# Relu and square of the summed quarters of fast up-projections, as two instructions or as one on VectorE

## The chip, the cores and the metric

The kernel runs on one core of a Trainium2 chip. The metric is the device time of one execution in microseconds (us). The engines are TensorE (PE, with its weight loads as PEld), VectorE (DVE), ScalarE (ACT), GpSimd (POOL) and SyncE (SP).

## The reference

Sliding-window attention with a linear position bias, followed by a feed-forward block whose activation is the square of a relu. There are 8 batches of 576 tokens, 8 heads of 64, a window of 128 keys, 2048 hidden features; inputs and output are f32.

```python
scores = scale * q @ k.T + slope[h] * -abs(rel)      # masked to 0 <= rel < 128
attn = softmax(scores);  x = (attn @ v) as [4608, 512]
h = x @ w_in                                          # [4608, 2048]
r = maximum(h, 0);  g = r * r
out = g @ w_out                                       # [4608, 512]
```

## The kernel before, in words

All products are in bf16 with f32 sums in PSUM. The attention goes by blocks of up to 128 tokens (40 blocks). POOL loads a block's keys, queries and values (L429); PE or a DMA transposes keys and queries; PE makes the scores (L533, L552); ACT takes exponentials (L598, L591); DVE multiplies them with a mask (L609, tile P); PE multiplies with the values (L639); DVE takes the reciprocal of the sum (L662) and normalises (L672, tile x); and x is transposed into xT, early by PE and DVE, later by a DMA on SP's queue (L686).

The feed-forward part goes by 9 groups of 512 tokens. An up-projection gives h transposed, features on partitions, and its activated form g is kept in SBUF as a tile of 16 x 512 columns, with two such tiles. The first two groups make their up-projection plainly (L745): ACT takes the relu out of the bank into a tile `rt` (L759), and DVE or ACT squares it into g (L767, L769).

The last 7 groups make it by a Strassen scheme with 7 products instead of 8 (`fast_unit`, L798 on). DVE first makes sums of the tokens' quarters (L789) and of the weights (L392). Each group has 4 units, so there are 28 units in all. A unit makes its 7 products (L820) in three PSUM banks A, B and C. ACT copies bank A out as `fs` (L880); DVE adds that into bank B (L886); ACT copies bank B out as `fu` (L890), and, after one more product, as `fx` (L901). The four quarters of h are then finished by `finish`:

- two quarters stand in a bank as they are: ACT takes the relu into an `rt` tile (L848), then DVE or ACT squares it into g (L869 or L871);
- two quarters need a sum more: DVE adds a bank and `fx` or `fu` into an `rt` tile in bf16 (L854), then DVE or ACT takes the relu in place (L859 or L861), then DVE or ACT squares it into g (L869 or L871).

There are three `rt` tiles. After each pair of units DVE makes the sums of the quarters of g (L934, tile S) that the output products need. These go by the same Strassen scheme (`product`, L975), with sums and copies of banks by DVE and ACT (L1004, L1033, L443, L445), and SP stores the result. The first group's output products are plain (L1054).

The order of all this is not that of the Python loops. Each piece of work is a task with a key (its place in the wanted order), with its dependences, with the buffers it takes and frees, and with a cost for each engine that may do it. `Plan.order` runs a list scheduler over these costs and gives each task its engine and its place; a task that may go to ACT or DVE goes to the one that can start it first. Every engine then works its instructions off in that order. `SPREAD` holds seeds of random draws, each with a size and a share: they shift the keys of some or all groups of tasks a little, and so choose one order among many. A negative share shifts the first loads.

Of the kernel before, what the change touches and what calls it, by code (L numbers as in the profile page):

```python
# [11 lines left out]
AF = mybir.ActivationFunctionType  # L12
ALU = mybir.AluOpType
# [188 lines left out]
def kernel(  # L202
    ctx: ExitStack, tc: tile.TileContext, q, k, v, moe_w_in, moe_w_out, out
):
    nc = tc.nc
# [5 lines left out]
    scale = 1.0 / (D ** 0.5)  # L211
# [48 lines left out]
    def overlap(e):  # L260
# [5 lines left out]
    plan = Plan({"rec": 4, "rt": 3, "g": 2, "S": 2, "S2": 1, "osb": 4,  # L266
                 "s1": 1, "u2": 1, "x1": 1, "fs": 1, "fu": 2, "fx": 1, **size},
                {"h": 3, "o": 3, "a": 4, "f": 5, "t": 3})

    def bank_tile(sl, name, dtype=FP32):  # L270
        return psum.tile([128, 512 if dtype == FP32 else 1024], dtype, tag=f"bank{sl.idx}", bufs=1, name=name)

    def act(n):
        return n * 0.836 + 50.0

    def dve(n, rate=1):
        return n / rate / 0.96 + 68.0

    def mm(n):
        return max(n, 64) / 2.4 + 4.0  # L280
# [515 lines left out]
    def fast_unit(g, n, key, t_of):  # L796
        if n == 0:
            g_slots[g] = Slot("g")  # L798
            g_sq[g] = [[] for _ in range(FCB)]
        sg = g_slots[g]  # L800
        x = xT[:, :, g * 512 % RING:g * 512 % RING + 512].rearrange("p (c k) (s t) -> p c s k t", c=2, s=2)
        bank = {x: Slot("f") for x in "ABC"}
        fs, fu, fx = Slot("fs"), Slot("fu"), Slot("fx")
        chain_ = {"last": None}

        def products(what, name, by, nth, after, end):
            opens = nth == 0
            for jj in range(2):
                for k in range(2):
                    def emit(jj=jj, k=k):  # L810
                        if opens and jj == 0 and k == 0:
                            bank[name].tile = bank_tile(bank[name], "f")
                        j = 2 * n + jj
                        if what[0] == "a":
                            r, c = int(what[1]) - 1, int(what[2]) - 1
                            w = w_in_sb[:, 2 * c + k, (2 * j + r) * 128:(2 * j + r + 1) * 128]
                        else:
                            w = w_sum[:, int(what[1]) - 1, k, j]
                        m = t_of(int(by[1]) - 1)[:, k] if by[0] == "t" else x[:, int(by[1]) - 1, int(by[2]) - 1, k]
                        nc.tensor.matmul(bank[name].tile[:, jj * 256:jj * 256 + 256], w, m,  # L820
                                         start=opens and jj == 0 and k == 0, stop=k == 1, skip_group_check=True)
                    new = jj == 0 and k == 0
                    chain_["last"] = plan.add(
                        {"PE": mm(256)}, key + 0.1 * (2 * jj + k), emit,
                        [chain_["last"], t_wsum[n] if what[0] == "s" else t_win[n][-1], t_tsum[g]] + (after if new else []),
                        ([bank[name]] if opens else []) + ([sg] if n == 0 and what == "a11" else []) if new else [],
                        [tsum[g]] if end and n == 3 and jj == 1 and k == 1 else [])
            t_read[g].append(chain_["last"])
            return chain_["last"]

        def f32(sl):
            sl.tile = work.tile([128, 512], FP32, tag=sl.tag, bufs=plan.bufs[sl.tag], name=sl.tag)
            return sl.tile

        def out(r, t):
            return sg.tile[:, 4 * n:4 * n + 4].rearrange("p (j r) (t q) -> p j r t q", r=2, t=2)[:, :, r, t]

        def finish(r, t, after, name, add=None):
            srt = Slot("rt")
            rel = [bank[name]]  # L840

            def two(x_):
                return x_.rearrange("p (j q) -> p j q", j=2)

            if add is None:
                def relu():
                    srt.tile = work.tile([128, 512], BF16, tag="rt", bufs=plan.bufs["rt"], name="rt")
                    nc.scalar.activation(srt.tile, bank[name].tile, AF.Relu, bias=0.0, scale=1.0)  # L848
                tr = plan.add({"ACT": act(512)}, key, relu, after, [srt], rel)
                t_sum_ = tr  # L850
            else:
                def plus():
                    srt.tile = work.tile([128, 512], BF16, tag="rt", bufs=plan.bufs["rt"], name="rt")
                    nc.vector.tensor_tensor(srt.tile, bank[name].tile, add.tile, op=ALU.add)  # L854
                t_sum_ = plan.add({"DVE": dve(512)}, key, plus, after, [srt], [add] + (rel if t == 0 or r == 0 else []))

                def relu():
                    if tr.eng == "DVE":
                        nc.vector.tensor_single_scalar(srt.tile, srt.tile, 0.0, op=ALU.max)  # L859
                    else:  # L860
                        nc.scalar.activation(srt.tile, srt.tile, AF.Relu, bias=0.0, scale=1.0)  # L861
                tr = plan.add({"ACT": act(512) + 42.0, "DVE": dve(512, 4)}, key, relu, [t_sum_])

            def square():
                if sg.tile is None:
                    sg.tile = work.tile([128, FCB, 512], BF16, tag="g", bufs=2, name="g")
                o, i = out(r, t), two(srt.tile)
                if ts.eng == "DVE":
                    nc.vector.tensor_tensor(o, i, i, op=ALU.mult)  # L869
                else:  # L870
                    nc.scalar.activation(o, i, AF.Square)  # L871
            ts = plan.add({"DVE": dve(512, 2), "ACT": act(512) + 42.0}, key, square, [tr], [], [srt])
            for jj in range(2):
                g_sq[g][4 * n + 2 * jj + r].append((256 * t, 256 * t + 256, ts))
            return t_sum_

        p1 = products("a11", "A", "b11", 0, [], False)

        def keep1():
            nc.scalar.activation(f32(fs), bank["A"].tile, AF.Copy)  # L880
        t1 = plan.add({"ACT": act(512)}, key, keep1, [p1], [fs])
        key += 4
        p6 = products("s2", "B", "t2", 0, [], False)

        def into():
            nc.vector.tensor_tensor(bank["B"].tile, bank["B"].tile, fs.tile, op=ALU.add)  # L886
        t6 = plan.add({"DVE": dve(512)}, key, into, [p6, t1], [], [fs])

        def keep2():
            nc.scalar.activation(f32(fu), bank["B"].tile, AF.Copy)  # L890
        t2 = plan.add({"ACT": act(512)}, key, keep2, [t6], [fu])
        key += 4
        p5 = products("s1", "C", "t1", 0, [], False)
        key += 4
        p2 = products("a12", "A", "b21", 1, [t1], False)
        finish(0, 0, [p2], "A")
        key += 4
        p7 = products("s3", "B", "t3", 1, [t2], False)

        def keep3():  # L900
            nc.scalar.activation(f32(fx), bank["B"].tile, AF.Copy)  # L901
        t7 = plan.add({"ACT": act(512)}, key, keep3, [p7], [fx])
        t22 = finish(1, 1, [p5, t7], "C", fx)
        key += 4
        p4 = products("a22", "B", "t4", 1, [t7], False)
        finish(1, 0, [p4], "B")
        key += 4
        p3 = products("s4", "C", "b22", 1, [t22], True)
        finish(0, 1, [p3, t2], "C", fu)
        if g >= PLAIN and n % 2:  # L910
            sums(g, n // 2, key)
# [157 lines left out]
    key = 0  # L1069
# [5 lines left out]
    for g in range(NG):  # L1075
# [15 lines left out]
        key = base + (64 if g == 0 else 128)  # L1091

    for (b, kb), t in t_xT.items():
        lo = b * S + kb * 128 - RING
        for g in range(NG):
            if g * 512 < lo + blk[kb] and g * 512 + 512 > lo:
                t.deps += t_read[g]

    SPREAD = ((78, 3, 1), (425, 16, 0.01), (451, 8, 0.01), (463, 8, 0.03), (537, 3, 0.1), (602, 1.5, -0.15),
              (705, 3, 0.03), (1454, 16, 0.03), (1463, 3, -0.15), (1578, 3, 0.03), (1611, 3, 0.01))  # L1100
    work_of = sorted({t.group for t in plan.tasks if t.group[1] > -100000})
    load_of = sorted({t.group for t in plan.tasks if t.dma and -900000 < t.group[1] < -800000})
    shift = dict.fromkeys(work_of + load_of, 0.0)
    for seed, most, share in SPREAD:
        draw = random.Random(seed)
# [51 lines left out]
```

## Time and profile before

| what | value |
|---|---|
| median of 3 runs | 291.49 us (291.4 to 292.12) |
| the profiled execution | 291.18 us, of which its span is 289.2 us |
| granted TensorE clock | 1.0 |
| instructions in the span | 9480 |
| POOL busy | 107.6 us |
| moved by DMA | 38.36 MB, 133 GB/s |

The span reaches from the first to the last instruction of the profile. An engine's busy time is the union of its instructions. In a group of instructions, a row gives line, engine and operation, what is written from what, the shape and the count; then the busy time of all, the mean duration of one in ns; and then the time that the engine sat idle just before them, with what ended it. PE's busy time is modelled, since matmuls overlap.

### The profile page before, as it was taken

The page shows a single profiled execution, that of the slowest core. Times are in us where ns is not written, and L with a number is a line of the kernel's source. Part 1 is how long each engine was busy: PE and PEld are TensorE (multiplying, and loading weights), DVE is VectorE, ACT ScalarE, POOL GpSimd, SP SyncE. Part 2 cuts the span into 40 slices and gives each one's busy share as a digit, 9 for nine tenths or more (in the row PEclk, how much of TensorE's full clock was granted, in tenths as well). Part 3 has the DMA queues.
Part 4 walks back from the last instruction along what each step waited for, and adds up shares of the span by engine and source line. Part 5 has one row for each costly group of instructions (what it writes and reads, how often), then busy time and mean ns, then how long its engine had stood idle before and what let it go on. Part 6 is the DMA issues. An engine that isn't in the chain of part 4 may idle for free.

```text
span 289.2 us, 9480 instructions
## 1 busy us (share of the span) xinstructions
PE 281.6 (97%) x3869; PEld 239.2 (83%) x3869; DVE 256.1 (89%) x625; ACT 229.1 (79%) x470; POOL 107.6 (37%) x134
## 2 busy tenths in 40 slices
PE   8899999999999999999999999999999999999995
PEld 6788878865788888888988888888888888888884
DVE  6876879999798999998999999989999988998823
ACT  6659888995489985999899989898879888588420
POOL 8958676944672516332634245332000000000000
PEclk9999999999999999999999999999999999999999
DMA  9999999999999999999999999999234101201223
GB/s 135 160 179 174 172 180 186 155 126 208 191 191 141 150 126 192 161 161 110 226 158 126 127 197 157 164 177 158 37 101 70 47 20 61 86 0 39 74 75 109
DMA packets 165867, 38.36 MB, mean 133 GB/s; under 512 B 153024, under 2 KB 165312, under 8 KB 165824
## 3 DMA queue, kind: packets, MB, share of 16 engines
q0 software_dynamic: 114704, 18.10, 92.3%
q1 hardware_dynamic: 50064, 19.41, 35.8%
q8 instruction: 30, 0.49, 0.7%
q10 hardware_dynamic: 1056, 0.26, 0.4%
q14 instruction: 13, 0.11, 0.1%
HBM read 36.70 MB, written 9.44 MB: 160 GB/s over the span
## 4 chain that ended last, share of the span: by engine, by line
PE 88%; POOL 4%; DMA 3%; DVE 2%; ACT 1%; issue 0%; DVEq 0%
PE o L975 33%; PE f L820 30%; PE h L745 8%; PE pv L639 6%; PE o L1054 5%; DMA w_in_sb<-in_moe_w_in_dram 3%; PE ps_s L533 3%; POOL kq L429 2%; PE ps_s L552 2%; POOL vt L429 1%; PE tp L483 1%; POOL w_in_sb L360 1%; PE xp L698 1%; DVE rt L854 1%; DVE g L869 0%
## 5 line engine op out<-in xcount | busy, mean ns | idle before, releaser
L429 POOL DMA_DIRECT2D vt<-in_v_dram x40 | 34.1, 854 | 66.5 <-PE pv L639 58.1
L598 ACT ACTIVATE E<-ps_s 128x384 bf16<-128x384 f32 (+2 forms) x114 | 50.5, 508 | 8.6 <-PE ps_s L533 8.6
L975 PEld LDWEIGHTS <-g 128*128 128x128 bf16 x512 | 49.1, 98 | 6.0
L820 PEld LDWEIGHTS <-w_sum 128*128 128x128 bf16 x448 | 43.1, 97 | 6.3 <-issue 0.5
L609 DVE TENSOR_TENSOR P<-E,masks 128x1024 bf16<-128x1024 bf16 (+1 forms) x67 | 43.5, 656 | 2.5 <-ACT E L598 1.6
L429 POOL DMA_DIRECT2D kq<-in_k_dram x39 | 33.2, 851 | 24.9 <-DMA kqT<-kq 17.5
L975 PEld LDWEIGHTS <-S 128*128 128x128 bf16 x384 | 36.6, 98 | 4.5 <-issue 0.4
L848 ACT ACTIVATE rt<-f 128x512 bf16<-128x512 f32 x56 | 33.2, 600 | 6.8 <-PE f L820 6.6
L975 PE MATMUL o<-w_out_sb,g 128*128 128x256 bf16 x256 | 38.3, 273 | 0.0
L975 PE MATMUL o<-w_mix,g 128*128 128x256 bf16 x256 | 37.2, 273 | 0.0
L745 PE MATMUL h<-xT,w_in_sb 128*128 128x128 bf16 (+1 forms) x384 | 35.3, 237 | 1.2 <-issue 0.6
L975 PE MATMUL o<-w_mix,S 128*128 128x256 bf16 x256 | 36.1, 273 | 0.2 <-ACT E L598 0.2
L820 PEld LDWEIGHTS <-w_in_sb 128*128 128x128 bf16 x336 | 31.8, 97 | 4.4
L820 PE MATMUL f<-xT,w_in_sb 128*128 128x256 bf16 x224 | 34.6, 273 | 0.0
L429 POOL DMA_DIRECT2D kq<-in_q_dram x39 | 33.4, 857 | 2.6 <-PE h L745 1.3
L871 ACT ACTIVATE g<-rt 128x512 bf16<-128x512 bf16 x52 | 32.6, 634 | 1.7 <-DVE rt L859 0.9
L820 PE MATMUL f<-xT,w_sum 128*128 128x256 bf16 x224 | 33.5, 272 | 0.2 <-DVE rt L854 0.2
L672 DVE TENSOR_TENSOR x<-pv,rec 128x256 bf16<-128x256 f32 (+1 forms) x80 | 33.0, 415 | 0.4
L820 PE MATMUL f<-T,w_sum 128*128 128x256 bf16 x224 | 32.1, 273 | 0.0
L639 PE MATMUL pv<-vt,P 128*128 128x65 bf16 x576 | 30.8, 193 | 0.9 <-DVE P L609 0.9
L639 PEld LDWEIGHTS <-P 128*128 128x128 bf16 x576 | 25.7, 97 | 6.1 <-DVE P L609 2.0
L745 PEld LDWEIGHTS <-w_in_sb 128*128 128x128 bf16 x384 | 26.7, 98 | 3.7 <-issue 1.0
(78 smaller groups left out, 504.1 us busy)
## 6 DMA issues: line engine op xcount, KB each, us to landing
out_dram<-osb SPq DMA_DIRECT2D x35, 256.0 KB, 3.7
vt<-in_v_dram POOLq DMA_DIRECT2D x32, 128.0 KB, 5.5
kq<-in_k_dram POOLq DMA_DIRECT2D x31, 128.0 KB, 6.0
kq<-in_q_dram POOLq DMA_DIRECT2D x31, 128.0 KB, 6.3
w_out_sb<-in_moe_w_out_dram POOLq DMA_DIRECT2D x4, 512.0 KB, 9.6
w_in_sb<-in_moe_w_in_dram POOLq DMA_DIRECT2D x6, 256.0 KB, 7.9
kq<-in_k_dram POOLq DMA_DIRECT2D x8, 64.0 KB, 5.7
kq<-in_q_dram POOLq DMA_DIRECT2D x8, 64.0 KB, 6.2
```

What stands on the lines that cost most here:

```text
L429: nc.gpsimd.dma_start(o, src[b, :, kb * 128:kb * 128 + n, :].rearrange("h s d -> s h d"))
L533: nc.tensor.matmul(sl.tile[lo:lo + 64, at:at + w], k[rows, c, unit:unit + 64], own[rows, C + c, q0:q0 + w], start=True, stop=True)
L598: nc.scalar.activation(o, src, AF.Exp, bias=0.0, scale=scale)
L609: nc.vector.tensor_tensor(Pt[sP.idx][:, hs, p0:2, 0:n], e, masks[:, hs, p0:2, 0:n], op=ALU.mult)
L639: nc.tensor.matmul(slot_v.tile[:, hi * (D + 1):(hi + 1) * (D + 1)], Pt[sP.idx][:, place(h), part, :], vt[s_in[mk, "v"].idx][:, h, :], star ...
L672: nc.vector.tensor_tensor(xt[sx.idx][0:n, hf * 256:(hf + 1) * 256].rearrange("p (h e) -> p h e", h=4), pv[0:n, :, 0:D], srec.tile[0:n, :]. ...
L745: nc.tensor.matmul(slot.tile[:, f * w:(f + 1) * w], w_in_sb[:, cc, (fc + f) * 128:(fc + f + 1) * 128], xT[:, cc, g * 512 % RING + lo:g * 5 ...
L820: nc.tensor.matmul(bank[name].tile[:, jj * 256:jj * 256 + 256], w, m, start=opens and jj == 0 and k == 0, stop=k == 1, skip_group_check=True)
L848: nc.scalar.activation(srt.tile, bank[name].tile, AF.Relu, bias=0.0, scale=1.0)
L871: nc.scalar.activation(o, i, AF.Square)
L975: nc.tensor.matmul(bank[t].tile[:, t * 256:(t + 1) * 256], left(g, what, j)[:, t * 128:(t + 1) * 128], right(by, j), start=opens and j == ...
L1054: nc.tensor.matmul(bank.tile, g_slots[g].tile[:, fc, t * 128:(t + 1) * 128], w_out_sb[:, fc], start=fc == 0, stop=fc == FCB - 1)
```

## The change

The relu and the square of the two summed quarters of a unit become one instruction of DVE, a scalar-tensor-tensor that takes the larger of the element and 0 and multiplies it with the element. It reads and writes bf16 in SBUF. The sum before it (L854) stays as it is. ACT can no longer be given these two steps. The planner counts the fused instruction as it counted the square on DVE. The other two quarters of a unit are finished as before. The list of random draws is another one, and has no entry with a negative share.

```diff
-                def relu():
-                    if tr.eng == "DVE":
-                        nc.vector.tensor_single_scalar(srt.tile, srt.tile, 0.0, op=ALU.max)
-                    else:
-                        nc.scalar.activation(srt.tile, srt.tile, AF.Relu, bias=0.0, scale=1.0)
-                tr = plan.add({"ACT": act(512) + 42.0, "DVE": dve(512, 4)}, key, relu, [t_sum_])
+                tr = None
 
             def square():
                 if sg.tile is None:
                     sg.tile = work.tile([128, FCB, 512], BF16, tag="g", bufs=2, name="g")
                 o, i = out(r, t), two(srt.tile)
-                if ts.eng == "DVE":
+                if tr is None:
+                    nc.vector.scalar_tensor_tensor(o, i, 0.0, i, op0=ALU.max, op1=ALU.mult)
+                elif ts.eng == "DVE":
                     nc.vector.tensor_tensor(o, i, i, op=ALU.mult)
                 else:
                     nc.scalar.activation(o, i, AF.Square)
-            ts = plan.add({"DVE": dve(512, 2), "ACT": act(512) + 42.0}, key, square, [tr], [], [srt])
+            ts = plan.add({"DVE": dve(512, 2)} if tr is None else {"DVE": dve(512, 2), "ACT": act(512) + 42.0},
+                          key, square, [t_sum_ if tr is None else tr], [], [srt])
...
-    SPREAD = ((78, 3, 1), (425, 16, 0.01), (451, 8, 0.01), (463, 8, 0.03), (537, 3, 0.1), (602, 1.5, -0.15),
-              (705, 3, 0.03), (1454, 16, 0.03), (1463, 3, -0.15), (1578, 3, 0.03), (1611, 3, 0.01))
+    SPREAD = ((4096, 8, 1), (4215, 3, 0.03), (4227, 3, 0.1), (4239, 3, 0.01), (4245, 3, 0.1), (4250, 16, 0.01),
+              (4261, 8, 0.03), (4294, 8, 0.01), (4307, 16, 0.03), (4528, 8, 0.01), (4593, 3, 0.03), (4902, 3, 0.1),
+              (4953, 3, 0.03), (4969, 8, 0.01), (5022, 3, 0.01))
```

Behind the two lines that the changed function loses, the line numbers of the changed kernel are lower by two: L886 becomes L884, L901 becomes L899, L934 becomes L932 and L975 becomes L973. The fused instruction has L864, and the plain squares of `finish` L866 (DVE) and L868 (ACT).

## The prediction

> **What bounds the kernel now.** I read the page first: its busy times, its forty slices and the engine shares of the chain that ended last.
>
> ```profile
> PE 281.6 (97%) x3869; PEld 239.2 (83%) x3869; DVE 256.1 (89%) x625; ACT 229.1 (79%) x470; POOL 107.6 (37%) x134
> PE   8899999999999999999999999999999999999995
> DVE  6876879999798999998999999989999988998823
> PE 88%; POOL 4%; DMA 3%; DVE 2%; ACT 1%; issue 0%; DVEq 0%
> ```
>
> TensorE (PE) is busy in 281.6 us of a span of 289.2 and holds 88% of the chain. It sets the end. But the slices show that VectorE (DVE) stands at nine tenths from the seventh slice to about the thirty-sixth, beside a PE that is just as full. So the second question is how much room DVE has in the stage where the changed instructions lie. They belong to the fast up-projections; the line of their squares on DVE tells when these run.
>
> ```profile
> L869 DVE TENSOR_TENSOR g<-rt x60: 389/420/426, 79.9 to 271.6; 128x512 bf16<-128x512 bf16 x60
> ```
>
> I asked for one window over the dense part, 80 to 260 us, and for three of the shorter windows at the two ends.
>
> ```profile
> 80.00:260.00 180.00, 179.59 (x2382) 155.41 (x2380) 172.71 (x396) 156.61 (x321) 50.99 (x61) 1.00 1.22 126
> ```
>
> ```profile
> 0.00:20.00 20.00, 17.45 (x300) 15.04 (x301) 14.72 (x48) 12.84 (x29) 16.50 (x25) 1.00 1.57 155
> 20.00:40.00 20.00, 18.89 (x408) 16.46 (x405) 15.09 (x40) 17.21 (x35) 15.55 (x20) 1.00 1.92 175
> ...
> 260.00:275.00 15.00, 15.00 (x139) 13.37 (x137) 12.96 (x25) 9.50 (x18) 0.00 (x0) 1.00 0.16 54
> ```
>
> The columns are PE, weight loads, DVE, ACT and POOL. From 80 to 260 us PE is busy in 179.59 of 180 us, so at most 0.41 us is to be won there. DVE is busy in 172.71 us and idle in 180 - 172.71 = 7.29 us. ACT has 23.4 us idle. The granted clock is 1.00. So the kernel is bound by PE with DVE 4% behind it, and ACT is the engine with room. PE's only larger idle time lies in the first 40 us: 2.55 + 1.11 = 3.66 us.
>
> **The change part by part.** What goes and what stays is read from the groups of the whole run, with the shapes kept apart, and from the groups of DVE in the window from 80 to 260 us.
>
> ```profile
> L871 ACT ACTIVATE g<-rt 128x512 bf16<-128x512 bf16 x52 | 32.6, 634 | 1.7 <-DVE rt L859 0.9
> L869 DVE TENSOR_TENSOR g<-rt 128x512 bf16<-128x512 bf16 x60 | 24.6, 419 | 3.2 <-ACT rt L848 2.5
> L861 ACT ACTIVATE rt<-rt 128x512 bf16<-128x512 bf16 x28 | 17.8, 640 | 3.9 <-DVE rt L854 3.7
> L859 DVE TENSOR_SCALAR rt<-rt 128x512 bf16<-128x512 bf16 x28 | 9.2, 330 | 0.6
> L767 DVE TENSOR_TENSOR g<-rt 128x512 bf16<-128x512 bf16 x12 | 5.1, 421 | 2.6 <-ACT rt L759 2.4
> ```
>
> ```profile
> L869 DVE TENSOR_TENSOR g<-rt 128x512 bf16<-128x512 bf16 x56 | 22.9, 418 | 1.6 <-ACT rt L848 0.8
> ...
> L854 DVE TENSOR_TENSOR rt<-f,fx 128x512 bf16<-128x512 f32 x26 | 17.8, 685 | 4.3 <-ACT fx L901 4.0
> L854 DVE TENSOR_TENSOR rt<-f,fu 128x512 bf16<-128x512 f32 x26 | 17.7, 680 | 0.3 <-PE f L820 0.3
> ...
> L859 DVE TENSOR_SCALAR rt<-rt 128x512 bf16<-128x512 bf16 x25 | 8.4, 335 | 0.5
> ```
>
> There are 28 units with two summed quarters each, so 56 relus (28 on ACT, L861, and 28 on DVE, L859) and 56 squares of them. The instruction order of the changed program has 56 fused instructions, all on DVE; no relu of a summed quarter; and of the 56 squares whose relu came straight from the bank, 21 on DVE (L866 there). At the squares of the first two groups it has 17 on DVE instead of 12. A few evictions change sides (DVE has two fewer). PE's work is the same but for three filler transposes; the loads, the transposes and the stores are as many as before, and the first 30 loads stand in the same order.
>
> On ACT this removes 28 relus and 22 squares of about 0.64 us, some 32 us of the 229. ACT is not the bound, so this is worth nothing by itself.
>
> On DVE I need the time that an instruction takes from a full queue, which is less than its duration, because the next one starts before it has ended. Two pieces of the timeline of DVE show it:
>
> ```profile
> 163.36 0.41 DVE L789 TENSOR_TENSOR T<-xT,T 128x512 bf16<-128x512 bf16 x1
> 163.69 0.68 DVE L609 TENSOR_TENSOR P<-E,masks 128x1024 bf16<-128x1024 bf16 x1
> 164.29 0.42 DVE L789 TENSOR_TENSOR xT<-xT 128x512 bf16<-128x512 bf16 x1
> ```
>
> ```profile
> 176.62 0.29 DVE L859 TENSOR_SCALAR rt<-rt 128x512 bf16<-128x512 bf16 x1
> 176.83 0.42 DVE L672 TENSOR_TENSOR x<-pv,rec 128x256 bf16<-128x256 f32 x1
> ```
>
> From start to start, a tensor-tensor on 128x512 bf16 takes 163.69 - 163.36 = 0.33 us (the square's shape), one of 0.68 us takes 164.29 - 163.69 = 0.60, and the tensor-scalar takes 176.83 - 176.62 = 0.21.
>
> **The price that the trace doesn't show** is that of a scalar-tensor-tensor on 128x512 bf16. The low end is the bf16 square, 0.419 us. The high end is the pair that it replaces, 0.330 + 0.419 = 0.749 us, for the same two operations on the same elements. Between them, with 512 elements, lie the rows of f32, such as the sum of L854 at 0.685. It is the nearest to the pair, and I take it: 0.60 us from start to start. The high end is 0.06 longer, 0.66, and the low end 0.33.
>
> [...]
>
> In the window, 52 of the 56 sums lie (26 + 26), so I put 52 fused instructions there. Out go 25 tensor-scalars, and of 56 plain squares all but about 20 (21 of the run's 60 stay), so 36.
>
> - added: 52 x 0.60 = 31.2 us
> - removed: 25 x 0.21 + 36 x 0.33 = 5.3 + 11.9 = 17.2 us
> - net: DVE needs 14.0 us more of a stage in which it idles 7.29 us
>
> So **14.0 - 7.3 = 6.7 us** don't fit. I count the idle time as usable in full, since most of it is waiting for ACT, which the change relieves:
>
> ```profile
> DVE rt L854 <- ACT fx L901: 4.0, 6, 0.9
> ...
> DVE g L869 <- ACT rt L848: 0.8, 2, 0.6
> ```
>
> It costs PE because DVE works in its fixed order, and what stands behind a fused instruction are the masks (L609), without which PE has no next value products; the sums into bank B (L886, then L884), without which ACT can't keep it and PE can't go on; the sums that free the banks; and the normalisations. The result of the fused instruction itself is not urgent. The wait that it has, for the sum two lines above, is for its own engine. There is no cover in the stage: PE is full, and each late mask or bank is a gap.
>
> Outside the window there is cover: the last units (260 to 275 us) add about 2 x 0.57 = 1.1 us, of 2.04 that DVE idles there, and after that nothing of the change is left. The squares that move to DVE before 80 us are 5 x 0.33 = 1.7 us, beside 10 us of idle DVE in the first 40; I set them at nothing. If that cover were gone they would cost at most the same 1.7. The new draws shift the order of all tasks by a few places; their own price is unknown, and I take zero, with 1.5 us to either side.
>
> The profiled execution took 291.18 us (span 289.2), 0.31 below the median of 291.49, which is no difference for this purpose. Forecast: 291.2 + 6.7 = **297.9 us**.
>
> **The rivals.**
>
> *The fused instruction runs at the rate of the bf16 square.* Then DVE gains 52 x 0.33 = 17.2 and loses 17.2 us: it is as full as before, ACT has 32 us less, DVE's waits for ACT shrink, and the little that PE loses could go. The point that decides is 14.0 turned into 7.3: (7.3 + 17.2) / 52 = 0.47 us from start to start. Below it nothing overflows. What there is to gain is 0.41 us in the window and the gaps at the start, the larger of which are these, in PE's timeline and in the chain:
>
> ```profile
> 22.18 1.52 PE L745 MATMUL h<-xT,w_in_sb 128*128 128x128 bf16 x23 [0.48 <-DMA w_in_sb<-in_moe_w_in_dram]
> ```
>
> ```profile
> 34.42 0.63 issue
> 35.05 1.18 PE h L745 x18
> ```
>
> Together 0.41 + 0.48 + 0.63 = 1.5 us: 289.7 us at best, 291.2 if the gaps stay, which hang on loads whose order is unchanged. This is the case on the faster side. For it speaks that input and output are bf16 with unit step, as in the square's row; against it, that the replaced pair takes 0.749.
>
> [...]
>
> [...]
>
> *None of the idle time is of use*, because DVE idles where it waits for PE and its lateness is handed on before the next gap comes: 291.2 + 14.0 = 305.2 us.
>
> **How the numbers follow.** The forecast, one element a cycle and an overflow, gets 0.65; its own range is 293 to 303 (with the high end of the price, 52 x 0.06 = 3.1 more, 301.0; with half of the idle time unusable, 3.6 more, 301.5; and below, with a few us of hidden room, 293). The fast rate gets 0.12, half of it below 290.6. The hidden case gets 0.15, of which 0.02 falls below 290.6, 0.11 within 0.3% and 0.02 above. The last rival gets 0.08. A measurement of this kernel can tell about 0.3% from no change, 290.6 to 292.4. So faster is 0.06 + 0.02 = 0.08, the same 0.06 + 0.11 = 0.17, slower 0.75. The range of 290.8 to 303 leaves out the lower part of the fast rate (0.07 with the hidden case's) and the last rival with a little of the forecast's upper edge (0.11).
>
> **What would show it.** The group of the fused instruction in the changed profile: 0.68 us is the forecast, 0.42 the first rival. In the window from 80 to 260 us (longer by then), DVE at 98% or more, PE below 98%, waits of PE and of its weight loads for DVE and ACT in place of the 0.41 us, and DVE's wait for the copies of bank B (L901, then L899) mostly gone. ACT should fall from 229 to about 198 us. The first 75 us should stay within 1.5 us of their length. If PE is still at 99% of the stage and the fused group at 0.68 us, the room in DVE was larger than its busy time tells, and the sum is wrong there; if the start has moved by several us, the new draws were not free.

## The result, and the profile after

The changed kernel takes 301.19 us (median of 4 runs, 300.26 to 302.06) against 291.53 us before (291.4 to 292.12): a ratio of 1.033, with a 95% interval of 1.029 to 1.036. It is 9.7 us slower; 6.7 were forecast. The profiled execution took 302.06 us, of which its span is 300.3. The granted clock was 0.998 in all four runs, so it can't explain 3%. These are the rows of its page that answer to those of before:

```profile
PE 286.0 (95%) x3866; PEld 238.6 (79%) x3866; DVE 269.3 (90%) x617; ACT 207.6 (69%) x422; POOL 107.6 (36%) x134
PE   7779999999999999999999999999999999999995
DVE  6847779999899998999999999999999998999733
DVE 43%; PE 34%; DMA 7%; ACT 6%; issue 5%; POOL 4%; DVEq 0%
```

PE was 88% of the chain that ended last; now DVE is its largest part. The group of the fused instruction, from the groups of the whole run:

```profile
L864 DVE SCALAR_TENSOR_TENSOR g<-rt 128x512 bf16<-128x512 bf16 x56 | 38.5, 687 | 0.7
```

It takes 0.687 us, the same as the f32 sums (0.685). Then the windows, with the columns PE, PEld, DVE, ACT and POOL:

```profile
0.00:20.00 20.00, 16.63 (x284) 14.05 (x285) 14.12 (x47) 12.39 (x29) 15.85 (x25) 1.00 1.54 151
20.00:40.00 20.00, 18.30 (x382) 16.29 (x379) 14.44 (x39) 15.47 (x33) 14.16 (x18) 1.00 1.85 163
...
80.00:260.00 180.00, 174.98 (x2311) 148.25 (x2309) 174.56 (x369) 132.81 (x269) 51.23 (x62) 1.00 1.23 126
```

From 80 to 260 us PE idles 5.02 us where it idled 0.41, and DVE idles 5.44 where it idled 7.29. Both engines now lose some 3%. How much longer the stage has become is shown by the first and the last sum into bank B, before (L886) and after (L884):

```profile
L886 DVE TENSOR_TENSOR f<-f,fs x28: 665/690/700, 77.5 to 265.9; 128x512 f32<-128x512 f32 x28
```

```profile
L884 DVE TENSOR_TENSOR f<-f,fs x28: 667/692/700, 80.7 to 277.8; 128x512 f32<-128x512 f32 x28
```

It is 197.1 us instead of 188.4, so 8.7 more. The two profiled spans differ by 11.1: these sums also start 3.2 us later, and what stands behind the last of them is 0.8 us shorter. In the first 40 us PE was busy in 34.93 us instead of 36.34. The same two stretches as windows:

```profile
77.50:265.90 188.40, 187.99 (x2472) 162.87 (x2465) 180.03 (x409) 163.95 (x336) 50.99 (x61) 1.00 1.20 124
```

```profile
80.70:277.80 197.10, 191.56 (x2455) 162.22 (x2453) 191.23 (x399) 144.07 (x290) 51.06 (x61) 1.00 1.12 118
```

PE's idle time grows by 5.1 us there, from 0.41 to 5.54. The other 3.6 us stand as busy time for the same products, which is modelled, so a wait need not show in full as a gap. What PE waits for in the stage is listed by its waits and by those of its weight loads, between 80 and 260 us:

```profile
PE pv L639 <- DVE P L609: 2.0, 8, 0.4
PE f L820 <- DVE rt L854: 1.5, 5, 0.4
PE f L820 <- DVE x L672: 0.6, 2, 0.3
PE f L820 <- ACT fu L888: 0.3, 1, 0.3
```

```profile
PEld L639 <- DVE P L609: 5.9, 14, 0.6
PEld L820 <- issue: 4.3, 12, 0.5
```

These are the waits of PE in the same window before, and of its weight loads those that answer to the two lines above:

```profile
PE o L975 <- ACT E L598: 0.2, 1, 0.2
PE f L820 <- DVE rt L854: 0.2, 1, 0.2
```

```profile
PEld L820 <- issue: 0.5, 3, 0.2
...
PEld L639 <- DVE P L609: 0.2, 1, 0.2
```

A few short waits have become many: for masks (tile P) and for the sums that free a bank, 0.6 us at the longest. One such wait can be followed in the timeline of DVE, and then of PE:

```profile
129.42 0.69 DVE L609 TENSOR_TENSOR P<-E,masks 128x1024 bf16<-128x1024 bf16 x1
130.02 0.69 DVE L864 SCALAR_TENSOR_TENSOR g<-rt 128x512 bf16<-128x512 bf16 x1
130.62 0.69 DVE L854 TENSOR_TENSOR rt<-f,fu 128x512 bf16<-128x512 f32 x1
131.22 0.17 DVE L662 RECIPROCAL rec<-pv 128x4 f32<-128x4 f32 x1
131.34 0.69 DVE L864 SCALAR_TENSOR_TENSOR g<-rt 128x512 bf16<-128x512 bf16 x1
131.95 0.68 DVE L609 TENSOR_TENSOR P<-E,masks 128x1024 bf16<-128x1024 bf16 x1
```

```profile
132.69 0.41 PE L639 MATMUL pv<-vt,P 128*128 128x65 bf16 x8 [0.37 <-DVE P L609]
```

Between the two masks of a block stand two fused instructions, 0.60 us each from start to start. The planner counted 0.33 for each, so the second mask comes 0.54 us later behind the first than planned, and PE's value products, which needed it at once, stand for 0.37 us.

### The profile page after: what moved, and what is told of

Its sections match the earlier page's. It is cut to its first block, busy times and chain, and to the rows that moved or that the text cites. A ratio compares the mean times of both kernels' runs of the same rounds, so it can differ in the third digit from the quotient of the medians.

```text
span 300.3 us, 9415 instructions
## 1 busy us (share of the span) xinstructions
PE 286.0 (95%) x3866; PEld 238.6 (79%) x3866; DVE 269.3 (90%) x617; ACT 207.6 (69%) x422; POOL 107.6 (36%) x134
## 4 chain that ended last, share of the span: by engine, by line
DVE 43%; PE 34%; DMA 7%; ACT 6%; issue 5%; POOL 4%; DVEq 0%
PE o L973 11%; DVE rt L854 9%; DVE g L864 6%; DVE S L932 6%; PE f L820 6%; PE h L745 6%; DVE P L609 6%; PE o L1052 5%; DMA kq<-in_q_dram 4%; DVE x L672 3%; DMA kq<-in_k_dram 3%; DVE f L884 3%; PE pv L639 3%; ACT fx L899 2%; DVE g L932 2%
## 5 line engine op out<-in xcount | busy, mean ns | idle before, releaser
L973 PEld LDWEIGHTS <-g 128*128 128x128 bf16 x512 | 48.7, 98 | 6.5 <-issue 0.3
L973 PEld LDWEIGHTS <-S 128*128 128x128 bf16 x384 | 36.6, 98 | 4.2
L864 DVE SCALAR_TENSOR_TENSOR g<-rt 128x512 bf16<-128x512 bf16 x56 | 38.5, 687 | 0.7
L973 PE MATMUL o<-w_mix,S 128*128 128x256 bf16 x256 | 37.9, 273 | 0.0
L973 PE MATMUL o<-w_mix,g 128*128 128x256 bf16 x256 | 37.9, 273 | 0.0
L973 PE MATMUL o<-w_out_sb,g 128*128 128x256 bf16 x256 | 35.4, 273 | 0.0
```

What stands on the lines that cost most here:

```text
L864: nc.vector.scalar_tensor_tensor(o, i, 0.0, i, op0=ALU.max, op1=ALU.mult)
L973: nc.tensor.matmul(bank[t].tile[:, t * 256:(t + 1) * 256], left(g, what, j)[:, t * 128:(t + 1) * 128], right(by, j), start=opens and j == ...
```

## The experiments

Two questions were to be told apart: whether DVE has too much to do, whatever its order, or whether PE loses because DVE takes longer than the order allows for; and what the new draws have to do with it. All times are medians of 4 to 10 runs. The kernel before took 291.8 to 291.9 beside them.

### The changed order, with another price in the same place

The instructions stand in the order of the changed kernel, and only what stands at L864 differs.

```diff
 # e4_square_only: leaves out the relu of the summed quarters
-                    nc.vector.scalar_tensor_tensor(o, i, 0.0, i, op0=ALU.max, op1=ALU.mult)
+                    nc.vector.tensor_tensor(o, i, i, op=ALU.mult)
 # e5_pair_in_place
-                    nc.vector.scalar_tensor_tensor(o, i, 0.0, i, op0=ALU.max, op1=ALU.mult)
+                    nc.vector.tensor_single_scalar(srt.tile, srt.tile, 0.0, op=ALU.max)
+                    nc.vector.tensor_tensor(o, i, i, op=ALU.mult)
 # e6_fused_and_square
                     nc.vector.scalar_tensor_tensor(o, i, 0.0, i, op0=ALU.max, op1=ALU.mult)
+                    nc.vector.tensor_tensor(i, i, i, op=ALU.mult)
```

> The changed kernel with its order kept, but a plain bf16 square in place of the fused instruction (the relu of the summed quarters is left out): 0.33 us from start to start instead of 0.60, so DVE has 52 x 0.27 = 14 us less to do in the stage. Theory of the DVE load: the time comes back to that of before, 291 to 293 us. Rival, the new order and the lighter ACT are what costs: it stays within 2 us of the changed kernel, 299 to 302 us.

Measured: 289.46 us, 0.992 of before (0.989 to 0.995). With the price that the planner counted, the new order is even a little faster than before, so in this order the whole loss, 11.7 us against this run, hangs on the 0.27 us by which the fused instruction is longer: 56 x (0.687 - 0.421) = 14.9 us of DVE, of which 11.7, or 79%, come through to the end. The window from 80 to 260 us of this run, and the group:

```profile
80.00:260.00 180.00, 180.00 (x2384) 157.21 (x2383) 173.16 (x387) 137.54 (x281) 50.97 (x61) 1.00 1.24 127
```

```profile
L864 DVE TENSOR_TENSOR g<-rt 128x512 bf16<-128x512 bf16 x52 | 21.9, 421 | 0.6
```

PE doesn't idle at all, beside a DVE that is busy in 173.16 us, 1.4 less than in the changed kernel. The run alone can't tell the two theories apart: it takes the price beyond the plan away, and with it as much load.

> The changed kernel with its order kept, but in place of each fused instruction the pair tensor-scalar and tensor-tensor, both on DVE: 0.21 + 0.33 = 0.54 us instead of 0.60, by the spacing before. Theory of the DVE load: 52 x 0.06 = 3 us faster than the changed kernel, about 298 us, although it has 56 instructions more. Rival, what counts is the number of instructions and their waits on one engine: as slow as the changed kernel or slower, 301 to 306 us.

Measured: 306.05 us, 4.9 above the changed kernel. My expectation was wrong by its sign, and the timeline of DVE tells why:

```profile
153.34 0.28 DVE L864 TENSOR_SCALAR rt<-rt 128x512 bf16<-128x512 bf16 x1
153.66 0.42 DVE L865 TENSOR_TENSOR g<-rt 128x512 bf16<-128x512 bf16 x1
```

The square waits for the relu just before it on its own engine. So the relu takes 0.32 us from start to start (0.33 in the median of the 56) and not the 0.21 that it takes where something else follows (in the kernel before, at 176.62 us), and the pair with the square's 0.34 some 0.66 or more. That is 0.06 us or more above the fused instruction, 56 times: 3.4 us or more, where 4.9 were measured. The rival's cause, the wait on one engine, was right.

> The changed kernel with its order kept and a second instruction behind each fused one, a bf16 square in place on the tile that was just read (its result isn't used): DVE has 52 x 0.33 = 17 us more to do in the stage. Theory that DVE is now the bound: nearly all of it shows, 316 to 319 us. Rival, PE still bounds and only some late masks and banks cost: half of it or less, 301 to 310 us.

Measured: 324.68 us, 23.5 above the changed kernel, or 0.42 us for each added square. More than the 17 us came through, because more was added: the square waits for the fused instruction, which so takes 0.72 us from start to start (median of the 56) instead of 0.60. With the square's 0.34 this is 0.46 us each, 26 us in all, of which 23.5 came through. At each of the three steps up from the planned price, most or all of DVE's added time reaches the end: this order gives little room beyond what was planned.

### The planner told the true price

```diff
-            ts = plan.add({"DVE": dve(512, 2)} if tr is None else {"DVE": dve(512, 2), "ACT": act(512) + 42.0},
+            ts = plan.add({"DVE": dve(512)} if tr is None else {"DVE": dve(512, 2), "ACT": act(512) + 42.0},
```

> The changed kernel with the planner told 0.60 us for the fused instruction instead of 0.33, so that the order allows for it. Theory of the DVE load: DVE has as much to do as before, and the time stays within 2 us of the changed kernel, 299 to 303 us. Rival, the time is lost because the order was planned with a wrong cost: most of the 10 us come back, 292 to 296 us.

Measured: 295.23 us, 1.013 of before (1.007 to 1.018). Six of the 9.7 us come back, with the same fused instructions. The plan also moves three plain squares and three copies of output banks (`osb`, L443) from DVE to ACT, from start to start 3 x 0.33 + 3 x 0.60 = 2.8 us. Even if all of that came through, some 3 us are left to the order, and for these the theory that DVE has too much to do falls. The window:

```profile
80.00:260.00 180.00, 176.64 (x2337) 152.54 (x2335) 176.23 (x373) 136.94 (x278) 51.06 (x61) 1.00 1.25 126
```

DVE is busier than in the changed kernel (176.23 instead of 174.56 us of the same 180), and PE too (176.64 instead of 174.98); over the whole run DVE is busy in 266.1 us instead of 269.3. PE's weight loads wait for masks 0.3 us instead of 5.9:

```profile
PEld L639 <- DVE P L609: 0.3, 1, 0.3
```

> The fused instruction planned with 0.60 us, with the draws of before: a second draw for the run with the true cost, which took 295.2 us. Theory that the wrong cost makes some 6 of the 10 us lost: 293.5 to 297 us, 5 us or more below the run with the same draws and the wrong cost. Rival, that run had a lucky draw: 299 us or more.

It has the draws of before beside the true price. Measured: 298.40 us, 5.2 below the 303.57 of the same draws with the wrong price (e1, below), as the theory had it; its own range of 293.5 to 297 was missed by 1.4. Here the plan moves 11 squares to ACT and takes three copies to DVE, 1.8 us net.

### The draws

Here `SPREAD` is exchanged: e1 is the changed kernel with the list of before, e2 the kernel before with the new list; e9 to e12 have an empty list (e9 the pair, e10 the fused instruction counted as 0.33, e11 counted as 0.60, e12 the square only).

```diff
-    SPREAD = ((4096, 8, 1), (4215, 3, 0.03),
...
+    SPREAD = ()
```

> The fused instruction with the random draws of before, and the planner's wrong cost of 0.33 us. Theory that the fused instruction and its wrong cost make the loss, whatever the draws: 299 to 304 us. Rival, the new draws are what costs: 291 to 294 us.

> The kernel before with the new draws alone: relu and square stay two instructions on DVE or ACT. Theory that the draws cost nothing: 290 to 293 us. Rival, the new draws make a worse order: 296 us or more.

Measured: e1 303.57 us, e2 296.89 us. The fused instruction is slow with the old draws too, so the new ones aren't what costs there. But they are not free: the pair, with the new list, is 5.1 us slower than with its own. The same groups are planned in another order, and with DVE busy in only 169.48 of 180 us PE idles 4.2:

```profile
80.00:260.00 180.00, 175.83 (x2327) 150.43 (x2326) 169.48 (x386) 150.97 (x309) 51.09 (x61) 1.00 1.24 128
```

> The kernel before with an empty list of draws: an order that nobody picked. Theory that an order not picked for its graph costs some 5 us (as the new draws do with the pair, 296.9): 295 to 298 us. Rival, the new draws were an unlucky list: 291 to 293 us.

> The changed kernel with an empty list of draws and the planner's cost of 0.33 us. Theory that the fused instruction beyond its planned cost makes the loss: 300 to 306 us, 4 to 8 us above the pair without draws. Rival, the fused instruction costs nothing where neither order is picked: within 2 us of the pair without draws.

> The fused instruction planned with 0.60 us, with an empty list of draws. Theory that planning with the true cost gives back 5 to 6 us (as with both lists of draws): 295 to 299 us, within 2 us of the pair without draws. Rival, the DVE load alone sets the time: as the fused one without draws, 300 us or more.

> The changed graph with an empty list of draws and a plain square in place of the fused instruction (the relu of the summed quarters is left out), so that DVE takes what the planner counts. Theory that DVE time beyond plan is what PE loses: 10 us or more below the fused one without draws, 289 to 294 us. Rival, an order that wasn't picked is slow whatever the instruction takes: 296 us or more.

Measured: e9 293.83, e10 300.26, e11 295.41, e12 291.93 us. e9 is 1.2 below its expected range: a list that nobody picked costs the pair 2 us, not 5. e12 is 8.3 us below e10, a little less than the 10 that were expected. All medians together, in us:

| what stands on DVE, and what the planner counts | list of before | new list | no list |
|---|---|---|---|
| pair, as before | 291.8 | 296.9 | 293.8 |
| fused, counted as 0.33 (the change: new list) | 303.6 | 301.2 | 300.3 |
| fused, counted as 0.60 | 298.4 | 295.2 | 295.4 |
| square only, counted as 0.33 | not run | 289.5 | 291.9 |

Read down a column. In the orders planned for 0.33, the step from the square to the fused instruction costs 11.7 and 8.3 us. Counting it right gives back 5.2, 6.0 and 4.9. The work that the plan moves off DVE explains 1.8, 2.8 and 1.7 of that by its price (five squares in e11), and by DVE's busy time of the whole run some 3 us each, so 2 to 3 us are left to the order. In all three orders the waits of the weight loads for masks, from 80 to 260 us, shrink with it: from 4.8 us to 1.8, from 5.9 to 0.3 and from 7.0 to 1.3. What is left of the fused instruction is 6.6 us above the pair with the list of before, 1.7 below it with the new one and 1.6 above it without. The last two are within the noise: the 95% intervals of these runs against before reach 0.6 to 1.7 us to either side.

### One more way

```diff
-            ts = plan.add({"DVE": dve(512, 2)} if tr is None else {"DVE": dve(512, 2), "ACT": act(512) + 42.0},
+            ts = plan.add({"DVE": dve(512), "ACT": 2 * (act(512) + 42.0)} if tr is None else {"DVE": dve(512, 2), "ACT": act(512) + 42.0},
...
+                if tr is None and ts.eng == "ACT":
+                    nc.scalar.activation(srt.tile, srt.tile, AF.Relu, bias=0.0, scale=1.0)
+                    nc.scalar.activation(o, i, AF.Square)
```

> The planner may put relu and square of a summed quarter on DVE as one fused instruction, at 0.60 us, or both on ACT, at 1.04 us; new draws. Its order has 36 fused instructions and 20 pairs on ACT, so that DVE has about 20 x 0.60 = 12 us less to do than with the true cost alone. Theory of the DVE load: PE is the bound again, 289 to 292 us, as good as before or a little better. Rival, waiting for ACT costs as much as it saves: 293 to 296 us.

Measured: 296.71 us, 1.017 of before (1.014 to 1.020). DVE is busy in 168.51 of the 180 us, less than in any other run with a fused instruction, and PE still idles 3.9:

```profile
80.00:260.00 180.00, 176.11 (x2330) 151.20 (x2326) 168.51 (x359) 150.83 (x308) 51.06 (x61) 1.00 1.30 127
```

This is 0.7 us above even the rival's range of 293 to 296. The rival's cause is there: of the 3.9 us, PE waits 2.3 for ACT's copies of bank B (L902 and L891 in this kernel).

```profile
PE f L820 <- ACT fx L902: 1.2, 2, 0.6
PE f L820 <- ACT fu L891: 1.1, 1, 1.1
```

Taking work from DVE does not by itself bring PE back to its bound. No version that computes the reference beat the kernel before.

## Why the prediction was right, and where it was wrong

**The direction and the price: right.** The fused instruction takes 0.687 us, for which the row of 0.685 was taken; from start to start 0.60, as in the timeline above. The first rival, the rate of the bf16 square, is out: with bf16 in and out, the fused instruction took 0.687 us, against 0.421 for the bf16 square (e4). The "one element a cycle" of the forecast's chances is a rate that no run shows; what the runs show in its place is the 0.687 us, beside 0.685 for the f32 sums. The "hidden case", in which the added DVE time would have found room, is out too: the time rose by 9.7 us, and from 80 to 260 us PE idles 5.02 us, where it idled 0.41.

**The counts: right.** The 56 fused instructions, the 21 and 17 squares and ACT's 48 fewer instructions are in the trace. ACT's durations, added up over all its instructions, fall from 268.8 to 237.4 us, by 31.4 where some 32 were forecast. Its busy time falls by 21.5 only, to 207.6 and not 198: what counts twice in the sum of durations, because an instruction starts before the one in front has ended, falls from 39.7 us to 29.8.

**Two terms were mis-sized, and their errors partly cancel.** From the first to the last sum into bank B, DVE's busy time grew from 180.03 to 191.23 us, by 11.2 and not by 14.0. Its idle time, "usable in full", fell from 8.37 to 5.87, by 2.5 and not in full. The difference is the 8.7 us by which the stage grew, where 6.7 were forecast. Part of the first error is the relu's price of 0.21, read at one place where something else follows: in the kernel before, a square starts 0.32 to 0.33 us behind 11 of its 28 relus on DVE, so some 11 x 0.11 = 1.2 us more went out than the sum says. What makes up the rest of the 2.8 stays open. The forecast of DVE at 98% of the window fails too: it is 97.0% (174.56 of 180). The wait for the copies of bank B did shrink, as forecast, from 4.0 us to 1.1, yet the masks were late elsewhere:

```profile
DVE rt L854 <- ACT fx L899: 1.1, 3, 0.5
```

**The mechanism behind it was only half right.** The sum said that 14.0 us don't fit into 7.3. But with the price planned in, the same fused instructions run with DVE at 97.9% of the window and 6.0 us faster, 2.8 to 3.2 of them beyond what the plan moved off DVE, and the run with a light DVE (e8) is no better than that. What the runs showed in place of a pure overflow is the last rival's mechanism, in part: an instruction longer than its order allows for delays the next mask or bank, and PE stands before DVE's next gap can make up for it. In the order planned for 0.33, of 14.9 us of such lateness 11.7 came through. That the planner counted 0.33 was known, and the forecast gave it no term. That a sum of busy times came within 3 us is partly luck. Besides the two errors above, it rests on two things that the runs show to be separate: 11.7 us for the price beyond plan, and 2.4 us to the good (291.9 to 289.5) for the new order at the planned price.

**The new draws at zero, with 1.5 to either side: wrong.** The same list moves the pair by 5.1 us. With the fused instruction the new list is 2.4 us faster than that of before (301.2 to 303.6), so a list has no price of its own apart from what it orders. The 0.41 us that PE lost before were not the kernel's nature but that order's.

**The start within 1.5 us: held by one mark, not by another.** PE's busy time of the first 40 us fell by 1.41, and from 40 to 80 us it has no gap, as before. Its largest gap waits for a load:

```profile
21.82 0.40 PE L483 MATMUL tp<-ident,kq 128*128 128x128 bf16 x4 [1.26 <-DMA kq<-in_q_dram]
```

In e4, e5 and e6, which have the same order there, PE was busy in 36.42, 35.72 and 34.85 us of the first 40. So the order doesn't set this loss; it differs by as much from run to run. These are the windows of e4:

```profile
0.00:20.00 20.00, 17.03 (x288) 14.37 (x289) 14.32 (x47) 12.59 (x29) 16.04 (x25) 1.00 1.56 154
20.00:40.00 20.00, 19.39 (x398) 16.88 (x399) 15.77 (x42) 16.30 (x34) 16.36 (x21) 1.00 1.92 174
```

The first sum into bank B, though, starts 3.2 us later than before, at 80.7 instead of 77.5, and in e4 at 79.1: so up to 1.6 us of that belong to the order, and the rest to that run.

**What stays open.** Three lists of draws are few. Whether a list picked for the true price would bring the fused instruction to 291.8 or below wasn't tried. With the true price, the fused instruction is still 3.4 us above the kernel before (295.2 to 291.8), and whether that is DVE's load or an order that could be better isn't shown. Nor is it settled what makes the order of before lose so little; that the load of DVE alone doesn't set the time is shown by e2, where DVE has less to do in the window than before and PE idles ten times as long.

## What to carry to other kernels

Before two instructions are made one, look at what each of them takes: here a tensor-scalar of 0.33 us and a square of 0.42 that could lie on two engines became one of 0.69 that can lie only on the fuller one. Where a planner sets the order, correct its price in the same edit: planning with a price that was 0.27 us too low in 56 places cost 5 to 6 us here, part of it because the right price also moves other work to the freer engine. On two lists of three that is more than what the instruction itself costs when it is counted right. And compare edits to such a kernel over more than one order, since a list of draws alone moved it by up to 5 us.

## What was not expected of the hardware

A tensor-scalar on 128x512 bf16 takes 0.21 us from start to start where an independent instruction follows (in the kernel before, at 176.62 us), and 0.32 where the next one reads its result (e5). So the pair back to back takes about 0.66, more than the fused instruction's 0.60. The same holds for the fused instruction, 0.60 and, with a square behind it that writes over its input, 0.72 (e6). In the kernel before, 13 of the 28 relus on DVE took 0.18 to 0.21 us and 11 took 0.32 to 0.33, with a square right behind; 28 more were on ACT. So here the pair is cheaper on DVE than the fused instruction only where its parts are set apart (0.21 + 0.33 = 0.54 us against 0.60) or given to two engines.
